# Mixing ahead of weight conversion, and m in column blocks and row groups, in a sparse attention plus MoE kernel

## The chip, the cores and the metric

The kernel runs on one core of a Trainium2 chip. The metric is the device time of one execution in microseconds (us). The median of three runs of the kernel before is 865.87 us (864.05 to 866.86). Its engines are called by their short names: PE (TensorE, matrix products; PEld is its weight load), DVE (VectorE), ACT (ScalarE), POOL (GpSimd) and SP (SyncE, which issues most transfers).

## The reference

Three stages in a chain, all in float32. Batch 4, 8 heads, 576 tokens, head size 64, so 2304 rows of 512.

```python
# 1 attention, top 32 of 576 scores per row
scores = q @ k.T / 8;  kth = 32nd largest of a row
attn = softmax(where(scores >= kth, scores, -1e9));  x = attn @ v
# 2 soft MoE: 8 experts with 4 slots each
logits = x @ phi                                   # 2304 x 32
d = softmax(logits, axis=tokens);  slots = d.T @ x # 32 x 512
slot_out[e] = relu(slots[e] @ w1[e]) @ w2[e]       # 512 -> 1024 -> 512
c = softmax(logits, axis=slots);  y = c @ slot_out # 2304 x 512
# 3 feed forward, 512 -> 2048 -> 512
h = y @ w_in
g = where(h >= 1, h, where(h <= -1, 0, (h + 1)**2 / 4))
out = g @ w_out
```

## The kernel before

Attention and the sums of stage 2 take the first 565 us; the change does not touch them, apart from line numbers. w_in is split and converted there and stands as eight tiles cv_d in device memory. w_in and w_out arrive as 64-bit words; a conversion turns them into float32.

Behind it lies the tail, whose order of work on PE, ACT, DVE and POOL is the order in which the code is written (lines 1041 to 1107). First the experts: `ex_in` (L830) is the product with w1, `ex_relu` and `ex_turn` clip and transpose it, `ex_out` (L853) the product with w2, four experts at a time in four column groups of PE; `ex_save` (L860) copies the result so, `ex_place` (L865, L869) transposes it and writes it to so128. In between, the mix coefficients c: `mix_split` (L806 on ACT, L807 on DVE) cuts a batch's c into a high and a low part, `mix_turn` (L816 on PE, L818 on ACT) transposes it into cT.

The tail then uses h = c @ (slot_out @ w_in). So m = slot_out @ w_in is computed once, and stage 3 takes it in 512-column parts. `m_first` (L883) makes the first part, for f = 0 to 3 (f counts 16 blocks of 128 of the 2048 columns of w_in); L885 (ACT) and L886 (DVE) cut it into high and low. `m_rest` (L892) makes the other three, each in its own 32 rows of one PSUM tile and its own column group of PE; `m_split` (L899, L900) cuts them, and `m_spread` (L908, L909) spreads one over 128 rows when it is needed.

A step is one block of 384 rows (t) and one f. There are 96 steps; the first 32 alternate between t = 0 and 1, so that each f lasts two steps. Step i computes h of step i+3 (L955 on PE, relu and square L957 and L958 on ACT), its g (L963 on DVE; L969 on ACT or L971 on DVE cast it, L975 on DVE takes the rest), and the nine output matmuls of its own g with w_out (L991). The PSUM pool that h, m and the transposes use has two buffers.

w_out is converted in the tail by `prep(f, k)` in five pieces: k = 0 is L937 and L938 on ACT; k = 1 L940 and L941 on DVE and L942 on POOL; k = 2 L944 on DVE, the last reader of the raw tile; k = 3 L947 on ACT; k = 4 L949 on DVE. The table `todo` says in which step a piece of f = 8 to 15 is issued; those of f = 0 to 7 stand in the written order.

The weight tiles are loaded through one SP queue in the order of the list `worder`: w1 and w2, with four w_out tiles (f = 0 to 3) in between, then cv_d and the other w_out tiles. A tile's place comes free when its reader is done; each load waits for its place and for the eighth load before it.

Of the kernel before, what the change touches and what calls it, by code (L numbers as in the profile page):

```python
# [47 lines left out]
SOON = 8  # L48
# [26 lines left out]
def kernel_body(tc, qT, kT, vP, phi, w1, w2, w_in, w_out, out, fast, flag):  # L75
# [42 lines left out]
    worder += [(2, 0, 0), (2, 0, 1)] + [(4, 0, f) for f in range(EARLY, SOON)]  # L118
    worder += [(2, 0, n) for n in range(2, 2 * NHP)] + [(4, 0, f) for f in range(SOON, NF)]
# [760 lines left out]
    def m_first():  # L880
        ps = ps_m.tile([P, 512], F32, name="m_ps0", tag="m_ps")
        for c in range(NHP):
            nc.tensor.matmul(ps, so128[:, c].rearrange("p g s -> p (g s)"), wtile[(2, 0, c // 2)][c % 2],  # L883
                             start=(c == 0), stop=(c == NHP - 1))
        nc.scalar.copy(m4[0], ps)  # L885
        nc.vector.tensor_tensor(m4[0][64:], ps[64:], m4[0][64:].bitcast(F32), op=ALU.subtract)  # L886

    def m_rest(n):
        if n == 1:
            mx["m"] = ps_m.tile([P, 512], F32, name="m_ps1", tag="m_ps")  # L890
        for c in range(NHP):
            nc.tensor.matmul(mx["m"][32 * n:32 * n + 32], so128[:, c, 0, :], wtile[(2, 0, 2 * n + c // 2)][c % 2],  # L892
                             start=(c == 0), stop=(c == NHP - 1), tile_position=(0, 32 * n), skip_group_check=True)
# [89 lines left out]
    def emit_o(t, f, rows):  # L983
# [4 lines left out]
        for n in rows:  # L988
# [4 lines left out]
            if f == NF - 1:  # L993
                o = ring_tile("o", o_slots, "o_sb", F32)[0]
                nc.scalar.copy(o, pos[t][n])
                nc.sync.dma_start(out[t * BLK + n * P:t * BLK + (n + 1) * P, :], o)

    todo = {}
    for f in range(SOON - 2, SOON):
        for k, lag in ((1, 0), (2, 1), (3, 1), (4, 2)):  # L1000
            todo.setdefault((f - SOON + 2 + lag, k), []).append(f)
    for f in range(SOON, NF):
        for k, lag in enumerate((0, 1, 2, 2, 3)):
            todo.setdefault((3 + 3 * (f - SOON) + lag, k), []).append(f)
    behind = []

    def step(i):
# [32 lines left out]
        emit_o(t, f, range(NS))  # L1040
# [3 lines left out]
    nc.vector.reciprocal(run_s, run_s)  # L1044
    ex_in(0, range(4))
# [133 lines left out]
```

## Time and profile before

| | us |
|---|---|
| median of the runs | 865.87 |
| profiled execution | 863.71 |
| its span in the trace | 861.9 |
| busy: PE, DVE, ACT, POOL | 817.4, 685.9, 645.1, 438.6 |
| attention and its sums | about 0 to 565 |
| experts, mix, m | about 565 to 640 |
| steps | 626 to 856 |

The span is what the trace covers; the 1.8 us between it and the time of the execution lie around it. All times below are counted from the span's start. A row of the timeline gives start, duration, engine, line, operation, output and input tiles, how many instructions it merges, and in brackets how long the engine was idle before it and what ended that. Neighbouring matmuls overlap, so a group's length is counted from the start of the first to the start of what follows.

### The profile page before, as it was taken

How to read it: one execution, taken by the hardware profiler on the slowest of the kernel's cores; microseconds unless marked ns; L12 is line 12 of the kernel's file. 1: busy time of each engine (PE TensorE's matmuls, PEld its weight loads, DVE VectorE, ACT ScalarE, POOL GpSimd, SP SyncE). 2: the span in 40 equal slices, each digit the busy share in tenths (PEclk: the TensorE clock that was granted, in tenths of full speed). 3: DMA queues.
4: the chain of work that ended last, by engine and by line, in shares of the span. 5: the costliest groups of instructions: out<-in, count | busy, mean ns of one | idle time of the engine just before them, and what ended most of it. 6: DMA issues, size and time to landing. Idle time of an engine off the chain costs nothing.

```text
span 861.9 us, 17740 instructions
## 1 busy us (share of the span) xinstructions
PE 817.4 (95%) x5695; PEld 677.2 (79%) x5695; DVE 685.9 (80%) x3109; ACT 645.1 (75%) x1298; POOL 438.6 (51%) x462
## 2 busy tenths in 40 slices
PE   4889999999999999999999999988689999999997
PEld 3678989988988989889889888733247888888885
DVE  6999999988999989899999896118377776666663
ACT  5688998988998988999988888325358875545452
POOL 2688888877788877788886867002111110000000
PEclk9799999999999999999999999989889999999999
DMA  8553563562552451542551633679950001101011
GB/s 237 154 159 97 163 185 95 167 183 75 144 143 72 122 144 57 135 118 83 142 131 54 175 127 110 257 253 405 408 216 1 1 19 56 38 0 38 1 37 40
DMA packets 45046, 108.60 MB, mean 126 GB/s; under 512 B 8240, under 2 KB 8240, under 8 KB 44944
## 3 DMA queue, kind: packets, MB, share of 16 engines
q1 hardware_dynamic: 44624, 106.73, 40.4%
q8 instruction: 47, 0.77, 0.4%
q10 hardware_dynamic: 320, 0.66, 0.3%
q14 instruction: 55, 0.45, 0.2%
HBM read 70.70 MB, written 8.91 MB: 92 GB/s over the span
## 4 chain that ended last, share of the span: by engine, by line
PE 85%; DVE 7%; DMA 5%; ACT 1%; issue 1%; POOL 0%; ACTq 0%; DVEq 0%; SPq 0%; POOLq 0%
PE o_ps L991 23%; PE s_ps L312 20%; PE av_ps L486 14%; PE pt_ps L458 7%; PE s_ps L414 4%; PE av_ps L487 3%; PE rem_ps L231 3%; DMA w<-cv_d 2%; PE moe_ps L576 2%; PE h_ps L955 2%; DMA w<-in_moe_w_dram 2%; DVE cand L339 2%; PE h L830 2%; PE xT_ps L535 1%; PE rem_ps L233 1%; DVE l L423 1%
## 5 line engine op out<-in xcount | busy, mean ns | idle before, releaser
L312 PE MATMUL s_ps<-kh,q 128*128 128x288 f32 x640 | 207.8, 342 | 16.5 <-DVE q L267 9.2
L991 PE MATMUL o_ps<-whl,ghl 128*128 128x512 f32 x864 | 217.0, 396 | 0.0
L446 POOL TENSOR_TENSOR ssb<-ssb,pen 128x576 f32<-128x576 f32 x141 | 180.5, 1285 | 18.2 <-ACT pen L443 15.8
L991 PEld LDWEIGHTS o_ps<-whl,ghl 128*128 128x128 f32 x864 | 162.4, 190 | 34.1
L312 PE MATMUL s_ps<-kl,q 128*128 128x288 f32 x640 | 181.0, 299 | 0.0
L339 DVE MAX8 cand<-ssb 128x8 f32<-128x82 f32 (+1 forms) x1008 | 164.3, 228 | 4.7 <-ACT ssb L330 3.8
L312 PEld LDWEIGHTS s_ps<-kh,q 128*128 128x128 f32 x640 | 123.6, 193 | 34.9 <-DVE q L267 9.5
L486 PE MATMUL av_ps<-v_sb,ptb 128*128 128x65 f32 (+1 forms) x1280 | 147.1, 261 | 0.4 <-ACT xT L548 0.4
L486 PEld LDWEIGHTS av_ps<-v_sb,ptb 128*128 128x128 f32 (+1 forms) x1280 | 141.1, 181 | 5.0 <-issue 2.9
L312 PEld LDWEIGHTS s_ps<-kl,q 128*128 128x128 f32 x640 | 124.4, 194 | 0.3
L423 DVE MAX8 l<-s_ps 128x8 f32<-128x576 f32 x144 | 109.2, 758 | 17.5 <-PE s_ps L414 17.0
L443 ACT ACTIVATE pen<-ssb,kb 128x576 bf16<-128x576 f32 x141 | 110.6, 795 | 3.3 <-POOL kb L439 2.1
L330 ACT COPY ssb<-s_ps 128x576 f32<-128x576 f32 x144 | 91.4, 642 | 25.1 <-PE s_ps L312 21.4
L449 ACT ACTIVATE ssb<-ssb,nm 128x576 f32<-128x576 f32 x141 | 109.2, 786 | 0.6 <-POOL ssb L446 0.6
L957 ACT ACTIVATE rg<-h_ps,half 128x384 f32<-128x384 f32 x96 | 55.8, 581 | 71.6 <-PE h_ps L955 71.4
L963 DVE SCALAR_TENSOR_TENSOR rg<-h_ps,rg 128x384 f32<-128x384 f32 x96 | 53.5, 557 | 52.8 <-ACT rg L958 52.8
L397 POOL TENSOR_SCALAR mb<-ssb,top 128x576 bf16<-128x576 f32 x48 | 83.3, 1735 | 17.1 <-DVE top L346 6.4
L942 POOL TENSOR_TENSOR tr_l<-tr_l 128x512 int32<-128x512 int32 x16 | 20.7, 1297 | 139.3 <-DVE tr_l L941 51.5
L468 ACT COPY ptb<-pt_ps 128x512 f32<-128x512 f32 x144 | 82.6, 599 | 3.8 <-PE av_ps L486 3.7
L458 PE MATMUL pt_ps<-ident,ssb 128*128 128x128 f32 x576 | 84.3, 273 | 0.3 <-ACT ptb L468 0.2
L399 DVE TENSOR_SCALAR_CACHE_REDUCE mb<-ssb,top 128x576 bf16<-128x576 f32 x96 | 75.8, 802 | 0.0
L346 DVE MAX8 top<-cand 128x8 f32<-128x56 f32 x432 | 73.6, 207 | 0.1
(160 smaller groups left out, 1309.2 us busy)
## 6 DMA issues: line engine op xcount, KB each, us to landing
w<-in_moe_w_dram SPq DMA_DIRECT2D x56, 512.0 KB, 6.7
q<-qst SPq DMA_DIRECT2D x60, 160.0 KB, 3.1
kh<-kst SPq DMA_DIRECT2D x60, 144.0 KB, 2.5
kl<-kst SPq DMA_DIRECT2D x60, 144.0 KB, 2.9
x<-in_moe_w_in_dram SPq DMA_DIRECT2D x16, 512.0 KB, 3.9
w<-in_moe_w_out_dram SPq DMA_DIRECT2D x16, 512.0 KB, 10.2
v_sb<-in_v_dram SPq DMA_DIRECT2D x16, 325.0 KB, 3.0
raw_t<-in_q_dram SPq DMA_DIRECT2D x15, 320.0 KB, 4.0
```

The source lines that it names most:

```text
L312: nc.tensor.matmul(s[:, hf, :HS], a, w, start=(n == 0), stop=(n == len(terms) - 1), skip_group_check=True)
L330: nc.scalar.copy(st[u]["ssb"][:, j], st.pop((u, j))[:, :, :HS])
L339: nc.vector.max(st[u]["cand"][:, j, 8 * g:8 * g + 8], row(u, j)[:, S * g // NSEG:S * (g + 1) // NSEG])
L397: nc.gpsimd.tensor_scalar(st[u]["mb"][:, j], row(u, j), t_u, None, op0=ALU.is_ge)
L423: nc.vector.max(st[u]["l8"][:, j], st.pop((u, j))[:, :, :HS])
L443: nc.scalar.activation(pen, row(u, j), AF.Relu, bias=st[u]["kb"][:, j:j + 1], scale=-BIG)
L446: nc.gpsimd.tensor_tensor(row(u, j), row(u, j), st.pop((u, "pen", j)), op=ALU.subtract)
L449: nc.scalar.activation(row(u, j), row(u, j), AF.Exp, bias=st[u]["nm"][:, j:j + 1], scale=0.125)
L458: nc.tensor.transpose(pt[:, c, :], pr[:, c * P:(c + 1) * P], ident)
L468: nc.scalar.copy(ptb, st.pop((u, "pt", j)))
L486: nc.tensor.matmul(o, pj[:, c, sl], v_sb[:, 4 * jj + c, :], start=(c == 0), stop=False)
L991: nc.tensor.matmul(pos[t][n], a[:, sl], w, start=(f == 0 and k == 0), stop=(f == NF - 1 and k == 2))
```

## The change

Five things are edited. In the written order of the tail, the pieces of mixing (`mix_split`, `mix_turn`) and of the experts stand first, and the pieces of the conversion of f = 0 to 3 behind them. The first part of m is made in two column blocks, 128 and 384 wide, in two PSUM tiles, and the first two h stand between the halves of the second block; step 0's output matmuls stand ahead of the h of step 3. The three other parts of m are made with the three column groups in turn. The conversions of f = 4 to 7 move from the order before the steps into the steps' table, one f each 2.25 steps from step 2 on, and all cv_d tiles are loaded ahead of w_out's f = 4 to 15. The last copy and transfer of the output are made in two halves, by ACT with ACT's queue and by DVE with SP's.

```diff
-    worder += [(2, 0, 0), (2, 0, 1)] + [(4, 0, f) for f in range(EARLY, SOON)]
-    worder += [(2, 0, n) for n in range(2, 2 * NHP)] + [(4, 0, f) for f in range(SOON, NF)]
+    worder += [(2, 0, n) for n in range(2 * NHP)] + [(4, 0, f) for f in range(EARLY, NF)]
...
-    def m_first():
-        ps = ps_m.tile([P, 512], F32, name="m_ps0", tag="m_ps")
+    def m_first(part, cs):
+        lo, hi = ((0, P), (P, 512))[part]
+        if not part:
+            mx[part] = ps_m.tile([P, P], F32, name="m_ps0", tag="m_ps")
+        elif cs[0] == 0:
+            mx[part] = ps_f.tile([P, 512], F32, name="m_ps3", tag="e_ps")[:, :hi - lo]
+        ps = mx[part]
+        for c in cs:
+            nc.tensor.matmul(ps, so128[:, c].rearrange("p g s -> p (g s)"), wtile[(2, 0, c // 2)][c % 2][:, lo:hi],
+                             start=(c == 0), stop=(c == NHP - 1))
+        if cs[-1] == NHP - 1:
+            nc.scalar.copy(m4[0][:, lo:hi], ps)
+            nc.vector.tensor_tensor(m4[0][64:, lo:hi], ps[64:], m4[0][64:, lo:hi].bitcast(F32), op=ALU.subtract)
+
+    def m_rest():
+        mx["m"] = ps_m.tile([P, 512], F32, name="m_ps1", tag="m_ps")
         for c in range(NHP):
...
+            for n in range(1, NC1):
+                nc.tensor.matmul(mx["m"][32 * n:32 * n + 32], so128[:, c, 0, :], wtile[(2, 0, 2 * n + c // 2)][c % 2],
+                                 start=(c == 0), stop=(c == NHP - 1), tile_position=(0, 32 * n), skip_group_check=True)
...
+                dst = out[t * BLK + n * P:t * BLK + (n + 1) * P, :]
+                if (t, n) == (NT // BLK - 1, NS - 1):
+                    a, z = slice(0, DM // 2), slice(DM // 2, DM)
+                    nc.scalar.copy(o[:, a], pos[t][n][:, a])
+                    nc.vector.tensor_copy(o[:, z], pos[t][n][:, z])
+                    nc.scalar.dma_start(dst[:, a], o[:, a])
+                    nc.sync.dma_start(dst[:, z], o[:, z])
+                else:
+                    nc.scalar.copy(o, pos[t][n])
+                    nc.sync.dma_start(dst, o)
...
-    for f in range(SOON, NF):
+    for f in range(EARLY, NF):
         for k, lag in enumerate((0, 1, 2, 2, 3)):
-            todo.setdefault((3 + 3 * (f - SOON) + lag, k), []).append(f)
+            todo.setdefault((2 + (f - EARLY) * 9 // 4 + lag, k), []).append(f)
...
+        if i == 0:
+            emit_o(t, f, range(NS))
         if nxt:
             emit_h(nxt)
...
-        emit_o(t, f, range(NS))
+        if i:
+            emit_o(t, f, range(NS))
...
-    m_first()
-    prep(5, 0)
+    m_first(0, range(NHP))
+    m_first(1, range(NHP // 2))
     emit_h(steps[0])
-    for k in (2, 3):
-        prep(4, k)
     emit_h(steps[1])
-    prep(5, 1)
+    m_first(1, range(NHP // 2, NHP))
     emit_g(steps[0])
```

What the new order is, at three places. In these rows c is a batch's mix coefficients before and cT after the transpose, c_ps the transpose's PSUM tile, so_sb the experts' result of four experts, tr_l a conversion's working tile, whl its result and w the raw tile. First ACT, around the copy of the first experts' result; the kernel before:

```order
L806 COPY c_9736<-ch 128x10x32
L947 CAST whl<-tr_l 128x512
L937 ACTIVATE tr_l<-w_9437 128x512
L938 ACTIVATE tr_l<-w_9437,two 128x512
L860 COPY so_sb<-so_9673 128x512
L818 CAST cT_9601<-c_ps 128x512
L818 CAST cT_9601<-c_ps 128x64
L806 COPY c_9768<-ch 128x10x32
L947 CAST whl<-tr_l 128x512 x2
L818 CAST cT_9602<-c_ps 128x512
L818 CAST cT_9602<-c_ps 128x64
```

The changed kernel at the same place:

```order
L804 COPY c_9730<-ch 128x10x32
L941 ACTIVATE tr_l<-w_9435 128x512
L942 ACTIVATE tr_l<-w_9435,two 128x512
L858 COPY so_sb<-so_9670 128x512
L816 CAST cT_9601<-c_ps 128x512
L816 CAST cT_9601<-c_ps 128x64
L804 COPY c_9757<-ch 128x10x32
L951 CAST whl<-tr_l 128x512
L816 CAST cT_9602<-c_ps 128x512
L816 CAST cT_9602<-c_ps 128x64
L941 ACTIVATE tr_l<-w_9437 128x512
```

The copies of so and cT (lines 860 and 818, now 858 and 816) come before the last conversions' results (line 947, now 951) instead of behind them; two of those stood ahead of the copies of cT for the third batch.

Second DVE, from the cut of the first part of m (L886, now L890, with m_0 the part) to the g of the second step (rg and ghl: g and its high and low parts); the kernel before:

```order
L886 TENSOR_TENSOR m_0_9418<-m_ps_9856,m_0_9418 64x512
L944 SCALAR_TENSOR_TENSOR tr_l<-w_9507,tr_l 128x512
L940 TENSOR_SCALAR tr_l<-tr_l 128x512
L941 TENSOR_SCALAR tr_l<-tr_l 128x512
L963 SCALAR_TENSOR_TENSOR rg<-h_ps,rg 128x384
L971 CAST ghl<-rg 128x384
L975 TENSOR_TENSOR ghl<-rg,ghl 128x384
L949 TENSOR_TENSOR whl<-tr_l,whl 128x512
L963 SCALAR_TENSOR_TENSOR rg<-h_ps,rg 128x384
L971 CAST ghl<-rg 128x384
L975 TENSOR_TENSOR ghl<-rg,ghl 128x384
```

The changed kernel at the same place:

```order
L890 TENSOR_TENSOR m_0_9418<-m_ps_9850,m_0_9418 64x128
L890 TENSOR_TENSOR m_0_9418<-m_ps_9857,m_0_9418 64x384
L967 SCALAR_TENSOR_TENSOR rg<-h_ps,rg 128x384
L975 CAST ghl<-rg 128x384
L979 TENSOR_TENSOR ghl<-rg,ghl 128x384
L967 SCALAR_TENSOR_TENSOR rg<-h_ps,rg 128x384
L975 CAST ghl<-rg 128x384
L979 TENSOR_TENSOR ghl<-rg,ghl 128x384
```

Four pieces of conversions stood among the first two g; none does now, and the cut of m is in two pieces ahead of the first g.

Third PE, at the other three parts of m (tile m_ps, 32 rows each; w is a cv_d tile); the kernel before:

```order
L892 MATMUL m_ps_9967<-w_9515,so_9543 32x512 x2
L892 MATMUL m_ps_9967<-w_9517,so_9543 32x512 x2
L892 MATMUL m_ps_9967<-w_9519,so_9543 32x512 x2
L892 MATMUL m_ps_9967<-w_9521,so_9543 32x512 x2
L892 MATMUL m_ps_9967<-w_9523,so_9543 32x512 x2
L892 MATMUL m_ps_9967<-w_9525,so_9543 32x512 x2
```

The changed kernel at the same place:

```order
L896 MATMUL m_ps_9939<-w_9507,so_9543 32x512
L896 MATMUL m_ps_9939<-w_9511,so_9543 32x512
L896 MATMUL m_ps_9939<-w_9515,so_9543 32x512
L896 MATMUL m_ps_9939<-w_9507,so_9543 32x512
L896 MATMUL m_ps_9939<-w_9511,so_9543 32x512
L896 MATMUL m_ps_9939<-w_9515,so_9543 32x512
L896 MATMUL m_ps_9939<-w_9509,so_9543 32x512
L896 MATMUL m_ps_9939<-w_9513,so_9543 32x512
L896 MATMUL m_ps_9939<-w_9517,so_9543 32x512
L896 MATMUL m_ps_9939<-w_9509,so_9543 32x512
L896 MATMUL m_ps_9939<-w_9513,so_9543 32x512
L896 MATMUL m_ps_9939<-w_9517,so_9543 32x512
```

Before, the two matmuls of one cv_d tile, and the two tiles of one column group, followed each other; now three column groups take turns.

## Rows read from the trace of the kernel before

**Rows 1.** Stretches: us; busy PE, PEld, DVE, ACT, POOL; granted clock; DMA share; GB/s.

```profile
602.00:606.00 4.00, 0.60 (x6) 0.38 (x9) 2.63 (x8) 1.86 (x4) 0.00 (x0) 0.60 1.06 393
606.00:612.00 6.00, 6.00 (x40) 1.64 (x35) 0.17 (x2) 0.77 (x3) 0.00 (x0) 0.70 1.02 406
...
619.90:623.20 3.30, 0.78 (x3) 0.30 (x2) 2.24 (x5) 3.02 (x6) 0.10 (x1) 1.00 1.03 410
623.20:630.00 6.80, 4.38 (x10) 3.31 (x11) 5.63 (x10) 4.69 (x9) 1.17 (x1) 0.50 1.03 411
```

**Rows 2.** Timeline 601.5 to 606: start, duration, engine, line, tiles, [idle before <-releaser].

```profile
604.30 0.62 ACT L947 CAST whl<-tr_l 128x512 fp32r<-128x512 f32 x1 [1.36 <-DVE tr_l L944]
...
605.45 0.37 PE L816 MATMUL c_ps<-ident,c 64*128 64x64 f32 x1 [3.40 <-ACT cT L818]
```

**Rows 3.** Transfers issued in 604.7 to 606: KB each, median us to landing.

```profile
w<-in_moe_w_dram SPq DMA_DIRECT2D x1, 512.0 KB, 7.5
```

**Rows 4.** Timeline 585 to 618, experts' product with w2, four column groups.

```profile
597.70 1.92 PE L853 MATMUL so<-w,h1T 128*32 128x512 f32 x16
...
612.36 0.16 PEld L853 LDWEIGHTS so<-w,h1T 128*32 128x32 f32 x5 [0.27 <-DMA w<-in_moe_w_dram]
```

**Rows 5.** Timeline of PE alone, 611.5 to 655.

```profile
616.36 3.70 PE L883 MATMUL m_ps<-w,so 128*128 128x512 f32 x8 [0.71 <-DVE so L869]
621.46 0.62 PE L955 MATMUL h_ps<-cT,m 128*128 128x384 f32 x2 [1.40 <-DVE m L886]
...
626.31 0.69 PE L955 MATMUL h_ps<-cT,m 128*128 128x384 f32 x1 [1.89 <-DVE rg L963]
...
626.79 3.75 PE L991 MATMUL o_ps<-whl,ghl 128*128 128x512 f32 x9
...
630.54 2.25 PE L991 MATMUL o_ps<-whl,ghl 128*128 128x512 f32 x9
632.73 7.11 PE L892 MATMUL m_ps<-w,so 128*32 128x512 f32 x24
639.77 0.44 PE L955 MATMUL h_ps<-cT,m 128*128 128x384 f32 x1
...
646.55 0.44 PE L955 MATMUL h_ps<-cT,m 128*128 128x384 f32 x1 [0.72 <-DVE rg L963]
...
648.92 0.34 PE L955 MATMUL h_ps<-cT,m 128*128 128x384 f32 x1
```

**Rows 6.** Timeline 617 to 655, DVE: cut of m, g of step 1.

```profile
620.72 0.69 DVE L886 TENSOR_TENSOR m<-m_ps,m 64x512 fp32r<-64x512 f32 x1 [2.89 <-ACT m L885]
...
625.70 0.55 DVE L963 SCALAR_TENSOR_TENSOR rg<-h_ps,rg 128x384 f32<-128x384 f32 x1
```

**Rows 7.** Timeline of ACT alone, 648.8 to 656.

```profile
650.34 0.50 ACT L969 CAST ghl<-rg 128x384 fp32r<-128x384 f32 x1
650.75 0.61 ACT L947 CAST whl<-tr_l 128x512 fp32r<-128x512 f32 x1
651.56 0.58 ACT L957 ACTIVATE rg<-h_ps,half 128x384 f32<-128x384 f32 x1 [0.20 <-PE h_ps L955]
652.17 0.53 ACT L958 ACTIVATE rg<-rg 128x384 f32<-128x384 f32 x1
652.60 0.65 ACT L937 ACTIVATE tr_l<-w 128x512 f32<-128x512 f32 x1
653.16 0.75 ACT L938 ACTIVATE tr_l<-w,two 128x512 f32<-128x512 uint32 x1
653.83 0.58 ACT L957 ACTIVATE rg<-h_ps,half 128x384 f32<-128x384 f32 x1
```

**Rows 8.** The output tile o_sb: instructions (ns min/median/max) and landing of its transfers.

```profile
L995 ACT COPY o_sb<-o_ps x18: 567/586/589, 708.6 to 856.1; 128x512 f32<-128x512 f32 x18
...
DMA to landing us min/median/max: 2.0/2.2/4.0
```

**Rows 9.** Groups by line in 585 to 640: busy us, mean ns.

```profile
L818 ACT CAST cT<-c_ps 128x64 fp32r<-128x64 f32 x4 | 0.9, 220 | 0.5 <-PE c_ps L816 0.5
```

More of the change, by code (lines that the diff above doesn't have):

```diff
@@ L47 @@
 EARLY = 4
-SOON = 8
 NCV = NHP * NC1 + NWE
@@ L878, in tell @@
             nc.vector.tensor_copy(flag, badm)
-    def m_first():
-        ps = ps_m.tile([P, 512], F32, name="m_ps0", tag="m_ps")
-        for c in range(NHP):
[L883 to L893, printed above, removed]
+    def m_first(part, cs):
[13 more added lines that the diff above has]
+        mx["m"] = ps_m.tile([P, 512], F32, name="m_ps1", tag="m_ps")
+        for c in range(NHP):
+            for n in range(1, NC1):
+                nc.tensor.matmul(mx["m"][32 * n:32 * n + 32], so128[:, c, 0, :], wtile[(2, 0, 2 * n + c // 2)][c % 2],
+                                 start=(c == 0), stop=(c == NHP - 1), tile_position=(0, 32 * n), skip_group_check=True)
     def m_split():
@@ L1016, in step @@
         if i == 2:
-            m_rest(1)
-            m_rest(2)
-            m_rest(3)
+            m_rest()
             mhl.extend(m_split())
@@ L1044, in kernel_body, with some @@
     nc.vector.reciprocal(run_s, run_s)
+    def some(f, *ks):
+        for k in ks:
+            prep(f, k)
     ex_in(0, range(4))
@@ L1050, in kernel_body @@
     nc.scalar.activation(mx["lt"], mx["lt"], AF.Exp)
-    prep(0, 0)
+    some(0, 0)
     mix_norm()
-    prep(0, 1)
+    some(0, 1)
     ex_in(1, range(2, 4))
     ex_relu(1)
-    prep(1, 0)
-    prep(1, 1)
+    some(1, 0)
     tell()
@@ L1060, in kernel_body @@
     mix_split(0)
-    for k in (2, 3, 4):
-        prep(0, k)
+    some(0, 2)
     ex_turn(1)
     mix_split(1)
-    prep(2, 0)
-    prep(2, 1)
+    some(0, 3, 4)
+    some(1, 1)
     ex_out(0, range(4, 6))
@@ L1069, in kernel_body @@
     mix_split(2)
-    for k in (2, 3, 4):
-        prep(1, k)
-    prep(3, 0)
-    prep(3, 1)
+    some(2, 0)
+    some(1, 2)
     ex_out(0, range(6, 8))
@@ L1077, in kernel_body @@
     mix_split(3)
-    for f in (2, 3):
-        for k in (2, 3, 4):
-            prep(f, k)
+    some(1, 3, 4)
+    some(2, 1)
     ex_out(1, range(2))
@@ L1083, in kernel_body @@
     mix_turn(2)
+    some(3, 0)
+    some(2, 2, 3)
     ex_out(1, range(2, 4))
     mix_turn(3)
+    some(2, 4)
+    some(3, 1, 2, 3, 4)
     ex_out(1, range(4, 8))
@@ L1088, in kernel_body @@
     ex_place(1)
-    prep(4, 0)
-    prep(4, 1)
-    m_first()
-    prep(5, 0)
+    m_first(0, range(NHP))
+    m_first(1, range(NHP // 2))
     emit_h(steps[0])
-    for k in (2, 3):
-        prep(4, k)
     emit_h(steps[1])
-    prep(5, 1)
+    m_first(1, range(NHP // 2, NHP))
     emit_g(steps[0])
-    prep(4, 4)
     emit_g(steps[1])
-    prep(6, 0)
-    for k in (2, 3):
-        prep(5, k)
     emit_h(steps[2])
-    prep(5, 4)
     emit_g(steps[2])
-    prep(7, 0)
     for i in range(len(steps) - NLAST):
```

5 lines of the change are left out of this document (removed).

## The prediction

> **What bounds the kernel now.** I read the stretches first, for busy shares, granted clock and DMA, then the waits inside the stretches where TensorE (PE) is not full, and the chain of waits last. Everything that the change touches lies behind 589 us of a span of 861.9. From 650 us on PE runs step after step without a gap, one step every 2.27 us (the spacing of two first activations, 651.56 and 653.83) [rows 7]; there only fewer instructions could help, and the change leaves those as they are. What is open lies between 600 and 650 us, in two parts.
>
> Up to 616 us the weights set the pace. The DMA queues move some 400 GB/s without a pause [rows 1], and the last tile of w2 is issued at about 604.8 and lands 7.5 us later [rows 3], at 612.3. PE's last wait for a weight ends at 612.36 [rows 4]. There is a visible stall before: at 605.45 PE has waited 3.40 us for a copy of the mix coefficients on ScalarE (ACT), which stands behind two conversions of w_out; the second, at 604.30, has itself waited 1.36 us for VectorE (DVE) [rows 2]. PE catches up on it before the last tile comes: it is busy 6.00 of 6.00 us from 606 to 612 [rows 1].
>
> From 616 us on no weight is late; the chain goes through ACT and DVE. m for the first f takes PE from 616.36 for 3.70 us, the first h only starts at 621.46, the first nine output matmuls at 626.79 [rows 5]. In 619.9 to 623.2 PE works 0.78 of 3.30 us, and in 623.2 to 630 the granted clock is 0.50, the lower of its two levels, 1.2 GHz [rows 1]. DVE's step for the second h, at 625.70, on which PE waits, stands behind conversions [rows 6]. At 632.73 the other three parts of m occupy PE for 7.11 us [rows 5].
>
> **The change, part by part.**
>
> Mix first. Nothing for the time. The stall of 3.40 us goes, but PE then waits for the tiles that land up to 612.3, and the work behind the last tile (so, its copy, the transposes) ends at 616.3 as before. What waits now is the conversion: the conversion of f=3 comes some 2 us later by the new order, and its raw tile's place is the one that the last w2 tile takes, so that SP's queue, and all cv_d tiles behind it, wait for DVE there. Cover: 7.5 us lie between issue and landing [rows 3], so the transfers ahead of it keep the engines busy unless it comes more than about 5 us later. I take 0, bounds 0 to +4 (that, or the clock case below).
>
> m in two column blocks, no conversion between. Before, 10.4 us lie between 616.36 and the first output matmul at 626.79 [rows 5]. Laid out anew: The first block is a quarter of the columns: 8 records, a quarter of 3.70 us, 0.9, so PE ends at 617.3; ACT's copy and DVE's subtract of 128 columns lie between the 0.22 of a 64-column copy [rows 9] and the 0.69 of the full subtract [rows 6], say 0.25 each: 617.9. PE meanwhile does half of the second block, 4 records of three quarters of 0.43: 618.6. Two h follow, 0.17 each, then the rest of the block, 1.3: 620.2, drained 620.5. ACT, two relu and two squares at 0.61 and 0.43 apart [rows 7], is free at 621.1 and copies the second block (0.45): 621.55; the subtract (three quarters of 0.69) ends at 622.1. Then max/min and cast of the first g, 0.5 and 0.4 (POOL has no conversion beside them now), and some 0.3 for the weight load: the first output matmul at 623.35. Gain 626.79 - 623.35 = 3.4 us. The clock: PE still idles between 620.5 and 622.6, so I let the first nine matmuls go at the lower clock, as before (3.75 us against 2.25 [rows 5]). Bounds: 2 (copies at their upper ends, some more waits) to 5.2 (clock stays up: 1.5 to 1.8 more).
>
> Three row groups in turn. Before: 24 records in 639.77 - 632.73 = 7.04 us, one column group after the other. The same kind of record with four groups in turn takes 1.92 us for 16 [rows 4], 0.43 per four. With three groups in turn that is 8 rounds of 0.43 = 3.45 us. Gain 3.5; bounds 0 (groups don't overlap) and 4.1 (24 records at 0.12). The cv_d tiles that it needs now come directly behind the first two, eight transfers of 1.28 us (512 KB at some 408 GB/s [rows 1]) behind 612.3, by 622.6; PE asks at 629.3.
>
> Split, spread and first steps. From the h behind m to the h three steps on, before 648.92 - 639.77 = 9.15 us [rows 5]; three steps alone would be 6.8, the rest are the split's copies and a wait until 646.55 for DVE, which had conversions of f=6 and 7 between. DVE now has only f=4 there. The split's two rounds and the spread stay: I lay it out at 8.4. Gain 0.7, bounds 0 to 1.2.
>
> Conversions of f=4 to 7 inside the steps. Twelve f now lie in steps 2 to 29, four per nine steps, where eight lay three steps apart. PE pays nothing, if ACT keeps up. ACT per nine steps: nine relu/square pairs (0.61 + 0.43), eight casts (0.41), four conversions (0.61 + 0.56 + 0.67) [rows 7]: 9.4 + 3.3 + 7.4 = 20.1 us, against 9 x 2.27 = 20.4 for PE, where before three steps held 5.8 of 6.8. So ACT is 98% full for 28 steps. Within nine steps it falls up to 1.8 us behind and regains it; PE asks for a g three steps (6.8 us) behind its h, and the chain h, relu, square, next step, cast, subtract takes some 4.4, so 2.4 us are cover. PE does not wait by that, with 0.6 us to spare at the tightest. I take +0.5 for waits of the ACT conversion on DVE and POOL that the row does not show; bounds 0 to +5 (every interval 10% longer: 20.1 becomes 22.1, 1.7 over PE per nine steps, three times).
>
> Last copy and transfer in halves. ACT's copy of 512 columns takes 0.58 at the end [rows 8]; a half lies between that and the 0.22 of 64 columns [rows 9], by the line through both 0.37. In the new order DVE's half waits for ACT's, so both end after about 0.8, and SP's issue comes 0.2 later than now, for half of the bytes; landing takes 2.0 to 4.0 us for 256 KB [rows 8]. I take 0, bounds -1.0 to +1.0 (ACT's queue has been idle since the start). The Trainium skill, PSUM — Partial Sum Buffer, section "PSUM bank collisions raise a hardware error", says that two engines must not read one bank at once; by that rule the halves can only run one after the other, as the order has it, and the split saves no copy time. No run here shows a collision.
>
> Sum: 0 + 3.4 + 3.5 + 0.7 - 0.5 + 0 = 7.1 us less. The profiled execution took 863.71 us (span 861.9), so it would take 856.6. The median of the runs is 865.87, 2.2 above the profiled one; the forecast for the median is 865.87 - 7.1 = 858.8.
>
> **Rivals.**
> 1. The clock stays at its upper level over the first steps, since of the pauses in front of the h of before, 1.40 and 1.89 us among them [rows 5], one of 2 us is left. 1.5 to 1.8 us more: 857.0.
> 2. PE waits for w2 between 602 and 612 instead of for ACT, and the clock is down when the last tile lands. For it: after the pause in 602 to 606 (0.60 us busy of 4) the clock fell, and 606 to 612 ran at 0.70 [rows 1]. Against: the tiles still bring PE a round every 1.28 us, more work than in that pause. Then so (1.9 us), transposes and m run at half speed: +4. 862.8. The Trainium skill, TensorE: Matmul & The Clock Gate, section "HAM oscillation — how this bites in real kernels", describes exactly waits for DMA between short bursts as what lowers the clock; by it this case would be likelier than I make it. The trace agrees for the one pause; no row shows what a wait with a round of work in it does.
> 3. ACT is the bound in steps 2 to 29: every interval 5 to 10% longer is 0.7 to 1.7 us per nine steps, 2.1 to 5.1 in all, 1.6 to 4.6 beyond what I took: 860.4 to 863.4. For it: 98% leave nothing for an interval that the row does not show.
> 4. Slower than before. The same place, decided by another mechanism: ACT's conversions wait for DVE and POOL in each f, and ACT stands while it waits. The slack is 1.5 us (0.3 per nine steps, three times, and the 0.6 to spare), so 0.13 us per f use it up, and from 0.8 us per f (12 x 0.8 = 9.6, less 1.5 and the 0.5 already taken) the whole gain is gone; at 1.0 us the time is 868.8. Against: in the steps of before, the conversion at 650.75 follows the cast at 0.41 without a wait [rows 7].
> 5. The three groups do not overlap, and m takes 7 us as before: 862.3. Against: the four-group rows [rows 4].
>
> **How the numbers follow.** Forecast 0.50 (its own range 857.3 to 860.3), rival 1 0.17, rival 2 0.10, rival 3 0.10, rival 4 0.05, rival 5 0.08. A measurement of this kernel can tell about 0.3%, 2.6 us, from no change, so faster begins at 863.3 or below: forecast, rivals 1 and 5 and most of 2 and 3, 0.88; same 0.08 from the rest of 2, 3 and 5; slower 0.04, of rival 4. The range for 8 in 10 runs from 855.8 (rival 1 with the end's gain) to 862.4 (rivals 5 and most of 3).
>
> **What would show it.** PE without the 3.4 us wait, and its last wait for w2 ending within 0.5 us of 612.4. First output matmul at about 623, the three-group m within 3.6 us and starting near 629.3, h three steps on at 641. From there 2.27 us per step; gaps of PE that end with DVE's subtract or ACT's cast speak for rivals 3 and 4. The lower clock in 606 to 618 would be rival 2, no lower clock at all behind 618 rival 1. I am wrong on the main term if the first output matmul does not come before 625.

## The result and the profile after

The changed kernel takes 855.38 us (median, 854.9 to 855.83), the kernel before, run with it, 864.96 (864.03 to 866.86): a ratio of 0.9886, 95% interval 0.9866 to 0.9907. Three later sets of runs give 864.03 to 864.09 for the kernel before, and one of them 856.17 for the changed kernel, run again; one run of the kernel before among them, of 4414.28 us, is left out. The profiled execution after took 855.83 us, its span is 854.0.

In the lists below, after's lines stand for lines of before with other numbers: L886 is m's first part (883), L889 and L890 its copy and cut (885, 886), L896 the other three parts (892), L959 h (955), L967 the g on DVE (963), L995 the outputs (991), L851 the experts' second product (853), L816 the copies of cT (818).

First the stretches of the changed kernel, in the columns of [rows 1] (the first two are the same times; the third is the first 18 output matmuls, the fourth the experts up to there).

```profile
602.00:606.00 4.00, 3.67 (x20) 1.07 (x20) 1.80 (x5) 1.32 (x3) 1.27 (x1) 1.00 1.04 400
606.00:612.00 6.00, 5.28 (x21) 0.92 (x18) 0.52 (x1) 0.00 (x0) 0.00 (x0) 1.00 1.03 408
...
621.84:628.26 6.42, 6.42 (x21) 4.77 (x20) 4.34 (x10) 3.21 (x6) 0.00 (x0) 0.73 1.03 410
568.10:622.60 54.50, 48.24 (x322) 17.02 (x315) 21.40 (x46) 20.88 (x42) 5.33 (x4) 1.00 1.01 394
```

PE is busy 3.67 of 4 us where it was 0.60, at a clock of 1.00, and then less busy than before from 606 to 612. The DMA moves the same 400 GB/s. Of these stretches only the first outputs, at 0.73, have some of the lower clock level, 1.2 GHz.

The timeline of PE alone, of the changed kernel, against [rows 2, 4, 5].

```profile
598.96 0.27 PE L814 MATMUL c_ps<-ident,c 64*128 64x64 f32 x1 [0.68 <-ACT cT L816]
...
611.02 1.90 PE L851 MATMUL so<-w,h1T 128*32 128x512 f32 x10 [0.23 <-DMA w<-in_moe_w_dram]
...
615.02 2.45 PE L886 MATMUL m_ps<-w,so 128*128 128x128 f32 x12 [0.71 <-DVE so L867]
...
621.53 0.41 PE L959 MATMUL h_ps<-cT,m 128*128 128x384 f32 x1 [2.43 <-DVE rg L967]
621.84 3.79 PE L995 MATMUL o_ps<-whl,ghl 128*128 128x512 f32 x9
...
626.07 2.27 PE L995 MATMUL o_ps<-whl,ghl 128*128 128x512 f32 x9
628.26 3.63 PE L896 MATMUL m_ps<-w,so 128*32 128x512 f32 x24
631.83 0.45 PE L959 MATMUL h_ps<-cT,m 128*128 128x384 f32 x1
...
640.27 0.34 PE L959 MATMUL h_ps<-cT,m 128*128 128x384 f32 x1
```

The wait of 3.40 us for the copies of cT is 0.68 us. PE's last wait for a weight ends at 611.02 (before 612.36), the first output comes at 621.84 (626.79), m's other parts start at 628.26 and take 3.57 us to the h behind them (7.04). Taken apart at these rows, with the last h (847.45 before, 839.23 after) and the span's end:

| stretch | before | after | gain |
|---|---|---|---|
| start to first m matmul | 616.36 | 615.02 | 1.34 |
| to first output matmul | 10.43 | 6.82 | 3.61 |
| to m's other parts | 5.94 | 6.42 | -0.48 |
| to the h behind them | 7.04 | 3.57 | 3.47 |
| to the h three steps on | 9.15 | 8.44 | 0.71 |
| to the last h | 198.53 | 198.96 | -0.43 |
| to the span's end | 14.46 | 14.74 | -0.28 |

The sum is 7.94 us, of which 6.60 lie behind the first m matmul. What holds up the third h at 621.53 is seen on ACT and DVE of the changed kernel (timeline 611 to 632; before: [rows 6]).

```profile
618.29 0.52 ACT L962 ACTIVATE rg<-rg 128x384 f32<-128x384 f32 x1
...
619.74 0.46 ACT L889 CAST m<-m_ps 128x384 fp32r<-128x384 f32 x1
620.24 0.56 DVE L890 TENSOR_TENSOR m<-m_ps,m 64x384 fp32r<-64x384 f32 x1 [3.43 <-ACT m L889]
620.83 0.56 DVE L967 SCALAR_TENSOR_TENSOR rg<-h_ps,rg 128x384 f32<-128x384 f32 x1
```

The first h has its square at 618.81, but DVE takes it up at 620.83 only: the second column block's cut, which waits for ACT until 620.24, stands ahead of it in DVE's order.

### The profile page after: what moved, and what is told of

Its sections match the earlier page's. It is cut to its first block, busy times and chain, and to the rows that moved or that the text cites. A ratio compares the mean times of both kernels' runs of the same rounds, so it can differ in the third digit from the quotient of the medians.

```text
span 854.0 us, 17761 instructions
## 1 busy us (share of the span) xinstructions
PE 817.9 (96%) x5703; PEld 677.6 (79%) x5703; DVE 679.2 (80%) x3103; ACT 647.7 (76%) x1307; POOL 438.7 (51%) x462
## 4 chain that ended last, share of the span: by engine, by line
PE 86%; DVE 7%; DMA 4%; ACT 2%; issue 1%; POOL 0%; ACTq 0%; SPq 0%; POOLq 0%; DVEq 0%
PE o_ps L995 23%; PE s_ps L310 20%; PE av_ps L484 14%; PE pt_ps L456 7%; PE s_ps L412 4%; PE av_ps L485 3%; PE rem_ps L229 3%; PE moe_ps L574 2%; PE h_ps L959 2%; DVE cand L337 2%; PE h L828 2%; DMA w<-in_moe_w_dram 1%; PE xT_ps L533 1%; PE rem_ps L231 1%; DVE l L421 1%; DMA w<-in_moe_w_out_dram 1%
## 5 line engine op out<-in xcount | busy, mean ns | idle before, releaser
L995 PE MATMUL o_ps<-whl,ghl 128*128 128x512 f32 x864 | 217.2, 396 | 0.0
L995 PEld LDWEIGHTS o_ps<-whl,ghl 128*128 128x128 f32 x864 | 161.8, 189 | 34.6 <-DVE ghl L979 0.3
L967 DVE SCALAR_TENSOR_TENSOR rg<-h_ps,rg 128x384 f32<-128x384 f32 x96 | 53.4, 556 | 50.8 <-ACT rg L962 50.8
```

The source lines that it names most:

```text
L995: nc.tensor.matmul(pos[t][n], a[:, sl], w, start=(f == 0 and k == 0), stop=(f == NF - 1 and k == 2))
```

## The experiments

Three lengths are compared. A is the time from the experts' first product (start) to the first m matmul; B from there to the span's end; the tail, a part of B, from the last matmul's end. Times of the span differ by chance ahead of these, as the first column shows; the intervals are those of the ratio to the kernel before in the same set of runs.

| kernel | start | A | B | tail | median | ratio, 95% |
|---|---|---|---|---|---|---|
| before | 566.69 | 49.67 | 245.55 | 5.85 | 864.96 | |
| before again | 565.12 | 50.28 | 245.59 | 5.89 | 863.42 | 0.998, 0.9964-0.9997 |
| changed | 565.57 | 49.45 | 238.95 | 6.13 | 855.38 | 0.9886, 0.9866-0.9907 |
| changed again | 568.16 | 49.88 | 237.99 | 6.29 | 856.17 | 0.9896, 0.9873-0.992 |
| 1 groups alone | 565.86 | 49.84 | 243.11 | 5.88 | 860.56 | 0.996, 0.9944-0.9977 |
| 2 one after another | 570.78 | 50.08 | 242.39 | 6.15 | 860.84 | 0.9967, 0.9946-0.9988 |
| 3 whole end | 566.56 | 50.29 | 238.33 | 5.86 | 857.26 | 0.9929, 0.9904-0.9954 |
| 4 one block | 564.97 | 50.31 | 238.44 | 6.07 | 857.3 | 0.9923, 0.9898-0.9949 |
| 5 mix order before | 564.99 | 50.40 | 239.16 | 6.30 | 856.23 | 0.9913, 0.9897-0.993 |
| 6 two tiles later | 565.58 | 47.34 | 241.79 | 6.54 | 856.45 | 0.9925, 0.9904-0.9947 |
| 7 first ghl ahead | 564.46 | 49.72 | 237.53 | 6.18 | 855.21 | 0.9904, 0.9887-0.992 |
| 8 both, whole end | 565.73 | 47.84 | 240.55 | 5.95 | 858.09 | 0.9943, 0.9922-0.9964 |
| 9 conversions in steps | 565.98 | 46.58 | 238.58 | 5.84 | 853.64 | 0.9876, 0.9853-0.9899 |
| 10 ghl ahead, whole end | 565.14 | 49.65 | 237.30 | 5.90 | 854.89 | 0.9897, 0.987-0.9925 |

**Before again and changed again**, both without an edit.

> The kernel before, unchanged, for its own scatter: where the time ahead of the first m matmul comes from chance, this profile's start of the first m matmul can lie anywhere from 614.2 to 616.9 us as in eight of the nine others, and from the first m matmul to the end it is 245.5 us again. The median of its times is 864.0 to 864.3, not 865.87. If the change itself moved the stretch ahead of it, it is 616.4 again.

> The changed kernel, unchanged, for its own scatter: from the first m matmul to the end 238.9 us again (0.2 either way), the start of the first m matmul anywhere from 614.2 to 616.9. Its median over this call's runs is 855.4 to 857.3: the other kernels built on it that measured no difference in their own stretches had 856.2 to 857.3. If the change itself brought the first m matmul forward, it starts at 615.0 again and the median is 855.4.

The kernel before has B 245.59, as it had 245.55, but its first m matmul lies at 615.40, 0.96 earlier than in its first profile; that of the changed kernel lies at 618.04, 3.02 later than in its first. The profile of the changed kernel run again is not quite like the others: outside the lower level its granted clock reads 0.95 where theirs reads 1.00, from 16 us to 852. Its last stretch at that value, in the columns of [rows 1]:

```profile
572.00:852.00 280.00, 271.41 (x1298) 196.21 (x1290) 176.35 (x357) 164.91 (x311) 20.98 (x16) 0.95 0.29 111
```

The kernel before alone, with 0.96 us between its two profiles, shows that the 1.34 us ahead of m need not come from the change. The column of starts says where most of it comes from: all fourteen profiles are of the same work up to there, and start between 564.46 and 570.78. In the two profiles of the kernel before it is the place of the lower clock just ahead of the start. The timelines of the first and of the second, at the same six matmuls of the sums of stage 2:

```profile
556.01 2.72 PE L576 MATMUL moe_ps<-xT,phi_sb 128*128 128x256 f32 x6
```

```profile
555.00 1.56 PE L576 MATMUL moe_ps<-xT,phi_sb 128*128 128x256 f32 x6
```

In the first, the lower level runs from 554.97 to 558.38 and the six take 1.16 us longer (granted clock of 555 to 558.4: 0.50, in the second 1.00); its experts start 1.57 later. The ratio of the kernel before to itself, 0.998 with an interval that leaves out 1, says that 0.2% is not told apart here: the interval does not hold all of the scatter.

**1, groups alone, and 2, one after another.** In kernel 1 the edit is made in the kernel before (whose outer loop stood in the calls), in kernel 2 it is taken back in the changed one:

```diff
-        for n in range(1, NC1):
-            for c in range(NHP):
+        for c in range(NHP):
+            for n in range(1, NC1):
                 nc.tensor.matmul(mx["m"][32 * n:32 * n + 32], ...
```

> The kernel before, with the three column groups of the later m blocks issued in turn and nothing else changed. Theory: the 24 matmuls of m_rest take about 3.6 us where they took 7.1, and nothing ahead of them moves, so the kernel is 3.5 us faster than before (near 861.5); the PE stall of some 3.4 us at 605 and the low clock behind it are still there. Rival A (the groups' order is worth little by itself, the stretch got shorter because conversions left it): m_rest still takes 6 us or more, gain under 1 us. Rival B (what is saved here is given back in the steps behind it, where ScalarE or VectorE would be late): m_rest takes 3.6 us but the gain at the end is under 2 us.

> The changed kernel, with the three column groups of m_rest issued one after the other again. Theory: m_rest takes 7.0 us in place of 3.6 and the kernel is 3.5 us slower than the changed one (near 858.9). Rival: the conversions of f = 4 to 7, which now lie in these steps, use the longer stretch, and half of the 3.5 comes back in the steps behind it: 1.7 us slower or less.

Kernel 1's PE:

```profile
626.14 4.04 PE L991 MATMUL o_ps<-whl,ghl 128*128 128x512 f32 x9
...
630.30 2.80 PE L991 MATMUL o_ps<-whl,ghl 128*128 128x512 f32 x9
633.03 3.63 PE L892 MATMUL m_ps<-w,so 128*32 128x512 f32 x24
636.59 0.45 PE L955 MATMUL h_ps<-cT,m 128*128 128x384 f32 x1
```

Kernel 2's PE:

```profile
634.03 7.11 PE L896 MATMUL m_ps<-w,so 128*32 128x512 f32 x24
641.07 0.45 PE L959 MATMUL h_ps<-cT,m 128*128 128x384 f32 x1
```

The order of issue alone makes 3.56 us of 7.04. In the single records, a matmul or a set that runs side by side starts every 0.43 us. One group after another, that makes 16 starts, at eight of which two matmuls begin together (634.47 and 634.48 in the kernel before), so that the groups overlapped there in part already; in turn it makes 8 starts of three (628.26, 628.27 and 628.28). Kernel 2's B is 3.44 above the changed kernel's: nothing comes back, its rival falls. Kernel 1's B falls by 2.44 only; 0.95 went ahead of m's other parts, where its lower clock ran from 624.65 to 631.48 and so over the second nine outputs (2.80 us for 2.25 in [rows 5]). That is the clock's place, not a wait behind.

**3, whole end.** The last copy and transfer as in the kernel before (the branch for the last block is taken out).

> The changed kernel, with the last copy and its transfer whole again. Theory: the halves are worth nothing, within 0.3 us, since VectorE's half starts when ScalarE's half is done. From the start of the last copy to the span's end it is 6.1 us in the changed kernel's profile and 5.8 in that of before; if the halves cost these 0.3 us it is 5.8 us here, if the halves save the difference of the copies' lengths (0.2 us) it is 6.3 us, and if both are within the landing's own scatter (2.0 to 4.0 us in the profiles) it can be anything from 5.5 to 8.

The changed kernel's end, timeline:

```profile
847.88 0.37 ACT L1002 COPY o_sb<-o_ps 128x256 f32<-128x256 f32 x1 [1.49 <-PE o_ps L995]
...
848.28 0.42 DVE L1003 COPY o_sb<-o_ps 128x256 f32<-128x256 f32 x1 [5.89 <-DMA out_dram<-o_sb]
848.73 0.33 SPq L1005 DMA_DIRECT2D out_dram<-o_sb  x1
```

DVE's half starts where ACT's ends, so the second transfer is issued 0.85 us behind the start of the copies; in the kernel before the whole copy starts at 856.10 and its transfer is issued at 856.71, 0.61 behind. The tail is 5.86 us here, and over all kernels 5.84 to 5.95 with the whole copy and 6.07 to 6.54 with halves. The seven profiles of each kind do not meet, and their means are 0.35 us apart: halves cost something, of the three outcomes named ahead the first. The time of this kernel (857.26) does not tell it.

**4, one block.**

```diff
-    m_first(0, range(NHP))
-    m_first(1, range(NHP // 2))
+    m_first()
     emit_h(steps[0])
     emit_h(steps[1])
-    m_first(1, range(NHP // 2, NHP))
```

> The changed kernel, with the first m block computed and copied whole again, the conversions of f = 4 to 7 still left in the steps. From the start of the first m matmul to the first output matmul it was 10.4 us before and is 6.8 us in the changed kernel. Theory: about 1.4 us of these 3.6 belong to the two blocks and the rest to the conversions that no longer stand in ScalarE's and VectorE's queues here: 8.2 us in this stretch, 1.4 us slower than the changed kernel. Rival A: the blocks made all of it: 10.4 us, 3.6 slower. Rival B: the conversions made all of it: 6.8 us, as fast as the changed kernel. All four kernels of this call have one and the same program up to the experts' products, so their profiles also show how much the time at which the experts' first product starts (566.69 us before, 565.57 after) and the time at which the last of the experts' weights lands (612.31 and 610.97) differ from one execution to the next: if these 1.3 us are chance, the four scatter over as much; if the change makes them, the three built on the changed kernel lie at 611.0 and the one built on the kernel before at 612.3.

Kernel 4's PE:

```profile
615.28 3.70 PE L881 MATMUL m_ps<-w,so 128*128 128x512 f32 x8 [0.71 <-DVE so L867]
620.38 0.62 PE L953 MATMUL h_ps<-cT,m 128*128 128x384 f32 x2 [1.41 <-DVE m L884]
...
623.04 2.50 PE L989 MATMUL o_ps<-whl,ghl 128*128 128x512 f32 x9
...
628.03 3.63 PE L890 MATMUL m_ps<-w,so 128*32 128x512 f32 x24
```

The first output comes 7.76 us behind the first m matmul, not 8.2: the blocks make 0.94 of the 3.61 us, the conversions that left make 2.67. But B is not longer. The clock did not fall here, and the nine outputs took 2.50 us for 3.79. The changed kernel, run again, did the same: 2.48 us.

```profile
618.04 2.51 PE L886 MATMUL m_ps<-w,so 128*128 128x128 f32 x12 [0.71 <-DVE so L867]
...
624.92 2.48 PE L995 MATMUL o_ps<-whl,ghl 128*128 128x512 f32 x9
...
629.90 3.79 PE L896 MATMUL m_ps<-w,so 128*32 128x512 f32 x24
```

From the first m matmul to m's other parts it needs 11.86 us, kernel 4 12.75, and the changed kernel's first profile, with the lower clock, 13.24. So where the clock stays up the blocks are worth some 0.9, and its fall costs some 1.4. The profile with 11.86 is the one at 0.95, so both may be a little more. Why the clock stayed up in kernel 4 is not shown.

**5, mix order before.** The written order of mix and of the conversion of f = 0 to 3 is put back; all else is as in the changed kernel.

> The changed kernel, with the order of mix and conversion of f = 0 to 3 from the kernel before. From the start of the experts' first product to the start of the first m matmul five profiles so far have 49.45 to 50.31 us, with either order. Theory: TensorE waits for the experts' weights there anyhow, so the stall of some 3 us for ScalarE near 605 comes back, with a stretch at the lower clock, and this length stays between 49.3 and 50.5 us; from the first m matmul to the end it is 238.3 to 239.0 us as in the other kernels with all of the rest of the change. Rival: mix first was worth 1 us or more, and this length is 51 us or more.

Kernel 5's PE:

```profile
602.66 0.36 PE L814 MATMUL c_ps<-ident,c 64*128 64x64 f32 x1 [3.40 <-ACT cT L816]
602.95 3.26 PE L851 MATMUL so<-w,h1T 128*32 128x512 f32 x16
...
611.39 1.90 PE L851 MATMUL so<-w,h1T 128*32 128x512 f32 x10 [0.23 <-DMA w<-in_moe_w_dram]
```

The stall of 3.40 us is back, 16 matmuls behind it take 3.26 us at the lower clock (1.92 in [rows 4]), and PE still ends waiting for the last weight. A is 50.40, 0.1 above the others' band of 49.45 to 50.31, and B 239.16. The four kernels with the order of before have A of 50.05 in the mean, the seven others with these loads 49.91. Mix first is worth 0.1 us, less than the scatter.

**6, two tiles later.** Two w_out tiles leave the place ahead of the experts' weights, and their conversions the stretch ahead of m:

```diff
-    worder[36:36] = [(4, 0, f) for f in range(EARLY)]
-    worder += [(2, 0, n) for n in range(2 * NHP)] + [(4, 0, f) for f in range(EARLY, NF)]
+    worder[36:36] = [(4, 0, f) for f in range(2)]
+    worder += [(2, 0, 0), (2, 0, 1)] + [(4, 0, f) for f in range(2, EARLY)]
+    worder += [(2, 0, n) for n in range(2, 2 * NHP)] + [(4, 0, f) for f in range(EARLY, NF)]
```

> The changed kernel, with the loads of f = 2 and 3 moved behind the experts' weights and the first two m tiles, and their conversions into the first steps. If landings bound the experts' second product, each tile ahead of the last weight costs its 1.27 us there: the length from the experts' first product to the first m matmul falls from 49.4 to 50.3 us to about 47.4, and the kernel is 2 to 2.5 us faster than the changed one, less up to 0.5 for the conversions in the first steps. Rival A: the product is bound by its order of turns and copies, not by the loads: 49.4 or more, no gain. Rival B: the length falls, but the conversions of f = 2 and 3 hold up the steps that use them, and from the first m matmul to the end it takes 2 us more than 238.3 to 239.0.

A is 47.34, 2.1 to 3.0 under the band, and with the start of the changed kernel (565.58 and 565.57) PE's last wait for a weight ends at 608.92 in place of 611.02. Two tiles of 1.28 us are 2.56: the landings bound this stretch. The edit also moves conversions out of this stretch, but kernel 5, which changes only the order of mixing and conversions, left A as it was. B is 241.79, 2.84 more, so rival B holds too and the time is the changed kernel's. The timeline of kernel 6 shows where, on PE, ACT, POOL and DVE:

```profile
608.92 1.90 PE L852 MATMUL so<-w,h1T 128*32 128x512 f32 x10 [0.23 <-DMA w<-in_moe_w_dram]
...
618.83 0.46 ACT L890 CAST m<-m_ps 128x384 fp32r<-128x384 f32 x1
...
620.62 0.66 PE L960 MATMUL h_ps<-cT,m 128*128 128x384 f32 x1 [3.61 <-DVE rg L968]
...
622.43 1.29 POOL L947 TENSOR_TENSOR tr_l<-tr_l 128x512 int32<-128x512 int32 x1 [29.84 <-DVE tr_l L946]
622.76 1.18 DVE L976 CAST ghl<-rg 128x384 fp32r<-128x384 f32 x1
```

ACT has a conversion's two pieces, from 617.65 to 618.93, ahead of the copy of m's second column block, which so starts 5.91 us behind the first m matmul (4.72 in the changed kernel). PE waits 3.61 us for the g behind it, the clock falls in that pause, for 6.83 us from 619.25 (3.41 in the changed kernel), and from the first m matmul to the first output it takes 1.33 us more. The slow cast behind it holds DVE 0.8 longer.

**7, first ghl ahead.**

```diff
-    m_first(1, range(NHP // 2, NHP))
     emit_g(steps[0])
+    m_first(1, range(NHP // 2, NHP))
     emit_g(steps[1])
+    emit_o(*steps[0], range(NS))
     emit_h(steps[2])
```

> The changed kernel, with VectorE's work for the first step ahead of the second column block's subtraction, and the first step's outputs ahead of the third h. In the changed kernel VectorE waits until 620.24 us for that block while the first step's square is done at 618.81. Theory: the first output matmul comes 5.0 to 5.3 us behind the first m matmul where it came 6.8 to 7.0, and from the first m matmul to the end it takes 236.9 to 237.6 us in place of 238.3 to 239.0, about 1.4 us faster. Rival: the h that now comes behind is late for step 2 and TensorE waits there instead: 238 us or more. The clock may decide with it: in three of four profiles it fell to the lower level for 3.4 us at the first outputs, in that of the whole block it did not, and that kernel made up 1.4 us by it; where it does not fall here, 235.5 to 236.5.

Kernel 7's PE:

```profile
614.18 2.45 PE L886 MATMUL m_ps<-w,so 128*128 128x128 f32 x12 [0.71 <-DVE so L867]
...
619.02 2.48 PE L995 MATMUL o_ps<-whl,ghl 128*128 128x512 f32 x9 [0.75 <-DVE ghl L975]
...
623.49 0.44 PE L959 MATMUL h_ps<-cT,m 128*128 128x384 f32 x1 [1.65 <-DVE rg L967]
...
625.96 3.63 PE L896 MATMUL m_ps<-w,so 128*32 128x512 f32 x24
```

The first output comes 4.84 us behind the first m matmul, and B is 237.53, as the theory has it, but not by its reason alone. The rival's wait is there as well (1.65 us for the h behind). From the first m matmul to m's other parts it takes 11.78 us, and the changed kernel took 11.86 where its clock did not fall (the profile at 0.95). What the order seems to give is that the pause of 2.43 us ahead of the first outputs becomes 0.75 and the clock stays up: in kernels 7 to 10 it did not fall there (in kernel 8 it fell at 624.42, in a later pause of 3.37). With the changed kernel's own order it fell in four profiles of five (the changed one, 2, 3 and 5); the fifth is the one at 0.95, so that none at 1.00 stayed up.

**8, both and the whole end, and 9, conversions in steps.** Kernel 8 has 6, 7 and 3 together. Of the ten pieces of f = 2 and 3, kernel 9 has seven in the steps' table where kernel 8 has three (the diff is against kernel 8, cut):

```diff
-    for i, k in ((1, 2), (1, 3), (2, 4)):
-        todo.setdefault((i, k), []).append(3)
+    for f, i, k in ((2, 0, 2), (2, 0, 3), (2, 1, 4), (3, 1, 1), (3, 2, 2), (3, 2, 3), (3, 3, 4)):
+        todo.setdefault((i, k), []).append(f)
...
     some(2, 0)
+    some(3, 0)
...
     emit_h(steps[2])
-    some(3, 0)
-    some(2, 2, 3)
     emit_g(steps[2])
-    some(3, 1)
-    some(2, 4)
```

> The changed kernel with both of the preceding edits and the last copy and transfer whole. From the last matmul's end to the span's end the six profiles have 6.07 to 6.15 us with halves and 5.85 to 5.88 whole, so 0.25 us less here. If the theory of both edits holds they add up: 2 to 2.5 and about 1.4 and 0.25, some 3.5 us faster than the changed kernel, near 851.7. Rival: the conversions of f = 2 and 3 meet the first steps' work on VectorE, where both edits want the same stretch, and the sum is under 2 us.

> As the kernel with both edits and the whole last copy, but the conversions of f = 2 and 3 stand inside steps 0 to 3, behind VectorE's work for the third h, so that no instruction that waits for GpSimd stands ahead of it. There TensorE waited 3.37 us for that work. Theory: the wait goes, from the first m matmul to the end it takes 237.3 to 238.2 us (the first ghl ahead has 237.5, the whole end saves 0.25, the conversions cost up to 0.9), and from the experts' first product to the first m matmul 47.3 to 47.9: about 2.5 to 3 us faster than the changed kernel in the sum of these two, which was 288.4. Rival: VectorE and GpSimd slow each other down here too, some step waits 1 us or more for a conversion, and the sum is 287 or more.

Kernel 8, timeline of DVE and PE:

```profile
623.46 0.69 DVE L949 SCALAR_TENSOR_TENSOR tr_l<-w,tr_l 128x512 int32<-128x512 int32 x1 [1.48 <-POOL tr_l L947]
...
624.67 0.69 PE L960 MATMUL h_ps<-cT,m 128*128 128x384 f32 x1 [3.37 <-DVE rg L968]
```

Kernel 9, timeline of PE:

```profile
612.56 2.45 PE L887 MATMUL m_ps<-w,so 128*128 128x128 f32 x12 [0.71 <-DVE so L868]
...
635.33 0.44 PE L960 MATMUL h_ps<-cT,m 128*128 128x384 f32 x1 [1.01 <-DVE rg L968]
```

In kernel 8 a conversion that waits for POOL stands ahead of the third h's step on DVE, and PE waits 3.37 us: A and B together are 288.39, nothing gained, its rival. In kernel 9 that wait is gone; A is 46.58, under what was expected, B 238.58, over it (a wait of 1.01 us at the spread is left). A and B together are 285.16 us, against 288.40 and 287.87 of the changed kernel: 2.7 to 3.2 us. Its median, 853.64, is the lowest of all and 2.5 under that of the changed kernel in the same set; the two intervals overlap, so the times alone do not show it, and of the lengths there is one profile.

**10, ghl ahead, whole end**, is 7 with 3.

> The changed kernel with the first ghl ahead and the last copy and transfer whole, the loads as in the changed kernel. From the first m matmul to the end 237.2 to 237.4 us where the clock stays up at the first outputs, 238.4 to 238.8 where it falls there for 3.4 us. The sum with the stretch from the experts' first product to the first m matmul (49.4 to 50.3) is 286.8 to 287.6, about 1.2 us under the changed kernel's 288.4. Rival: the whole end's 0.25 us was the scatter of the landings, and the last matmul's end to the span's end is 6.0 us or more here.

B is 237.30 and the tail 5.90, as expected.

## Why the prediction was right or wrong

**Its base was wrong.** The sum of the steps was 7.1 us. Against the profiled execution it put the time at 856.6; that execution took 855.83, and the medians are 855.38 and 856.17. The step that failed is the last one, "the forecast for the median is 865.87 - 7.1": it took the median of three runs of the kernel before, two of them over 865.8, as its time and moved the forecast up by 2.2. The kernel before has medians of 864.03 to 864.96 in four sets of runs and 863.42 as a kernel of its own; of its 59 runs 10 are over 865.8, and the median of all is 864.03. Its runs of the last set lie in two clumps, nine from 862.9 to 864.3 and six from 866.5 to 868.7; what makes the upper one stays open. On 864.03 the same sum gives 856.9.

Of the 3.4 us between 858.8 and 855.38, 2.2 are this offset. Another 0.45 is that the changed kernel's median lies under its profiled execution and not over it. The last 0.8 lies between the two profiles: 1.34 ahead of m, which is scatter, less the 0.5 by which the terms behind it came out short. Without that scatter the sum would have been 0.5 too large for the profile, not 0.8 too small. The range, whose lower end of 855.8 also stood on that base (its parts, 857.0 less 1.0, give 856.0), held nothing for such a scatter.

**Mix first: 0.** Right, by kernel 5. PE waits for weights instead, and rival 2, which would have made the time 862.8, fell: from 568.1 to 622.6 the clock is 1.00 through all of those waits of 0.22 to 0.33 us, with a round of work between. In the pause of 3.40 us it fell in all four profiles that have it ([rows 1, 2], before again, kernels 1 and 5). The Trainium skill, TensorE: Matmul & The Clock Gate, section "HAM oscillation — how this bites in real kernels", tells of a kernel that falls to the lower clock where its work between two waits for DMA is shorter than the wait. Here each wait was far shorter than the work, so the section does not speak of this case, and the prediction read it too widely.

**m in column blocks: 3.4.** 3.61 to the first output, of which kernel 4 gives 2.67 to the conversions that left and 0.94 to the blocks; 0.48 goes back since one more h now lies between the first outputs and m's other parts. It stands at 3.1. The reason given for it holds in kind; the prediction did not part the blocks from the conversions, and most of it is the conversions. Rival 1, the clock that stays up, did not come in the first profile and came in the second, which ran at 0.95; whether it comes at 1.00 in this order is not shown.

**Three groups in turn: 3.5.** 3.47 in the changed kernel, 3.47 and 3.48 by kernels 2 and 1. Rival 5 fell.

**Split, spread and first steps: 0.7.** 0.71. The wait of 0.72 at 646.55 [rows 5] for DVE is gone. It is there in kernel 1, which leaves the conversions where they were (9.18 us for 9.15); those of f = 6 and 7 that stood there were in the steps' table already, four pieces of each.

**Conversions inside the steps: -0.5.** -0.43, but not by the reason given. All profiles that make the change have 201.31 to 201.41 us from the h behind the first spread to the last h, where both of the kernel before and kernel 1 have 200.90 to 200.93. So rivals 3 and 4 fell. The 0.5 was a guess for waits of ACT on DVE and POOL. The steps that got longer (3.23 us for 2.99 up to the h at 657.09, 2.44 for 2.26 up to that at 701.26) hold waits of PE that end with DVE: in the first, a conversion's last piece (L953) stands ahead of the g in DVE's order, in the second PE waits for L953 itself. That the size fits is luck. The timeline of the changed kernel, PE's weight loads and DVE:

```profile
655.88 0.68 DVE L953 TENSOR_TENSOR whl<-tr_l,whl 128x512 fp32r<-128x512 f32 x1
...
656.49 0.55 DVE L967 SCALAR_TENSOR_TENSOR rg<-h_ps,rg 128x384 f32<-128x384 f32 x1
...
657.09 0.19 PEld L959 LDWEIGHTS h_ps<-cT,m 128*128 128x128 f32 x1 [0.58 <-DVE rg L967]
...
698.55 0.69 DVE L953 TENSOR_TENSOR whl<-tr_l,whl 128x512 fp32r<-128x512 f32 x1
...
699.29 1.70 PEld L995 LDWEIGHTS o_ps<-whl,ghl 128*128 128x128 f32 x8 [0.28 <-DVE whl L953]
```

**Halves at the end: 0.** They cost 0.28 here, within the bounds: both copies take 0.85 us one after the other, and the shorter transfers did not make it up.

Altogether the terms came to 6.60 of 7.1 behind the first m matmul in the first profile, and to 7.6 in the second, where the clock did not fall (245.55 or 245.59 against 237.99).

## What to carry to other kernels

Put the sum of the steps on the execution whose trace it was worked out from, and give the range the scatter of the stretches that the change does not touch; a median of three runs can lie 2 us off. Matmuls with 32 columns pay when the column groups take turns in the order of issue; here three groups did, as four do in [rows 4]. In an engine that works in order, ask of each moved instruction what waits behind it: taking the conversions out of the queues made more than splitting m, and putting two of them ahead of one step took all of a gain back.

## What the runs showed of the hardware that was not expected

A cast on DVE of 0.36 us took 1.18 when POOL's add ran beside it in kernel 6 (both rows above): it began 0.33 behind the add and ended 0.22 behind its end. Kernel 9 has the same:

```profile
626.92 1.27 POOL L947 TENSOR_TENSOR tr_l<-tr_l 128x512 int32<-128x512 int32 x1 [4.50 <-DVE tr_l L946]
...
627.25 1.16 DVE L976 CAST ghl<-rg 128x384 fp32r<-128x384 f32 x1
```

The tail has 14 such casts in six of the profiles, three of them in the kernel before (at 632.41 one of 1.16 us). They begin 0.33 to 0.99 behind the add and take 0.69 to 1.18, and all 14 end 0.22 behind its end. That looks like a block until the other's instruction is over, not a slower rate. The Trainium skill, SBUF — State Buffer, section "SBUF: two separate sides", says that the two engines share a pair of ports by an exclusive lock; the rows of the casts agree. In the changed kernel none of the 72 casts ran beside an add, and none took over 0.364 us. Its g (L967), which reads PSUM, took the same 0.56 us beside an add, in all of twelve places.

The clock's lower level comes at least once in every profile between 545 and 575 us, where PE has short work, and with one and the same program the experts start between 564.46 and 570.78; the latest is kernel 2, where the lower level held 13.65 us from 549.62 and came again at 566.69. The 0.95 of one profile is a value beside the two levels. There m's other parts took 3.72 us for 3.57, but from the h three steps on to the last h it was 199.04 for 198.96: the steps did not follow the clock.
